# Five buffers instead of three for raw weights, and one place in SBUF for two sets of tiles, in a top-k attention kernel with two MLPs

## The chip, the cores and the metric

The kernel runs on one core of a Trainium2 chip. The metric is device time in microseconds (us), lower is better. The engines are TensorE (PE, with its weight loads as PEld), VectorE (DVE), ScalarE (ACT), GpSimd (POOL) and SyncE (SP); in this kernel SP issues all DMAs from one queue, in order, and each engine works through its own instructions in order.

## The reference, cut to what matters

Attention over 4 batches, 8 heads, 576 positions of 64 values, in which each row of scores keeps its 32 largest entries; then two MLPs (512 to 2048 to 512) on the 2304 rows that come out. All values are float32.

```python
scores = scale * np.matmul(q, k.transpose(0, 1, 3, 2))
kth = np.partition(scores, -32, axis=-1)[..., -32:-31]
scores = np.where(scores >= kth, scores, -1e9)
attn = softmax(scores)
x = np.matmul(attn, v)                      # laid out as 2304 rows of 512
h = x @ w_in;   x = (h - np.tanh(h)) @ w_out        # first MLP
h = x @ w_in2;  x = elu(h) @ w_out2                 # second MLP
```

## The kernel before, in words

The 2304 rows are cut into six chunks of 384. For each chunk the kernel computes eight groups of attention tiles (48 groups in all) and then the chunk's two MLPs in 32 steps (m is the MLP, ft one of 16 slices of 128 hidden columns). The attention of chunk c+1 runs beside the MLPs of chunk c. A group's scores are matmuls into PSUM (L332 to L335) that ACT copies out (L336); the top 32 of each row are found on DVE in four rounds of MAX8 (L357) and three of MATCH_REPLACE8 (L371), and one DVE instruction masks and sums (L378). PE transposes the result (L399), ACT copies it (L400), PE multiplies with v (L421). A step of an MLP is `first` (matmuls h, L528, then on ACT the tanh, L531, or the relu and exp, L533 and L534), `gate` (g on DVE, L542 or L547, then `split` into a high and a low part gh and gl, on ACT and POOL, L140 and L141) and `second` (matmuls acc, L564).

**Raw weights.** The weights arrive as 64-bit words that each hold two float32 values, and they are prepared once, on the way into chunk 0. `prepare` (L166) takes one half of one (m, ft): 128 x 512 raw words, 4 KB in each of 128 partitions, 512 KB in all. It loads them into a tile `raw` (L171 and L172, named wr in the trace; three buffers, RAW_BUFS); ACT scales and rounds the low words (L182), POOL multiplies (L184), ACT scales the high words (L186, or L181 into a PSUM bank while that is free, which holds for the first 22 of the 64 halves); DVE joins both into `w` (L187, named wf, two buffers), which is the last reader of `raw`; ACT and POOL split `w` into a weight tile (L191, named wp; 5 buffers for half 0, 6 for half 1), and the weight tile is stored to DRAM (L192). From chunk 1 on the prepared weights are loaded from there (L203). Eight (m, ft), 12 to 19, are prepared early, and chunk 0 loads them from DRAM as well (EARLY, PREP_AT, PREP_RATE); the other 24 are prepared in the order in which chunk 0 needs them, and their weight tiles go straight to PE.

**Parked groups.** While chunk 0's attention runs alone, the scores of groups 16 to 23 are computed as well and parked in DRAM (`park`, L307: tile `s`, named sp, two buffers; its q and k in qp and kp, one buffer each), to be loaded again when their turn comes. `park` is traced with a lowered priority (`later`).

**The order of the work.** The program is written in ticks, four to a group. `before`, `mid`, `late` and `ends` say in which tick the loads, the scores, the transposes and the rest of a group are written; chunk 0's MLPs begin in tick 36, and each step writes one `load_next`, which is either `prepare` or a load of prepared weights. That order gives priorities only: a planner (TileContext with a simulated timeline) takes the written instructions by priority, hands out the buffers of each tag, and lays down the fixed order of every engine's queue and the waits. An instruction can come long before its tick where its data and buffers are free by the planner's simulation, so preparation runs ahead as far as its buffers let it.

Tiles live in SBUF pools. Before the change all of them but two constants lie in one pool, `sb`, each tag with its own place for the whole program.

Of the kernel before, what the change touches and what calls it, by code (L numbers as in the profile page):

```python
# [19 lines left out]
P = 128  # L20
B, H, S, D = 4, 8, 576, 64
# [7 lines left out]
NF = DFF // P  # L29
# [14 lines left out]
NMAX = max(SIZES)  # L44
# [7 lines left out]
EARLY = range(12, 20)  # L52
PREP_AT = 8
PREP_RATE = 2.5
AHEAD = 6

PARTED = 2
# [11 lines left out]
PARK_BUFS = 2  # L69
# [2 lines left out]

WI_BUFS = 5
WO_BUFS = 6
RAW_BUFS = 3
G_BUFS = 3
T_BUFS = 3
QR_BUFS = 2
KR_BUFS = 2
# [8 lines left out]
G_BUFS = 3  # L88
T_BUFS = 3
# [9 lines left out]
NU = 384  # L99
# [8 lines left out]
def tile_topk_attention_two_mlps(  # L108
# [9 lines left out]
    nc = tc.nc  # L118

    def pool(name, bufs, space=None):  # L120
        kw = {} if space is None else {"space": space}
        return ctx.enter_context(tc.tile_pool(name=name, bufs=bufs, **kw))

    const = pool("const", 1)
    sb = pool("sb", 2)
    ps = pool("ps", 1, PSUM)
    dr = pool("dr", 1, DRAM)

# [20 lines left out]
    def bank(tag, name, bufs):  # L149
        return ps.tile([P, 512], F32, tag=tag, name=name, bufs=bufs)  # L150
# [8 lines left out]
    weights, loads = {}, [(ci, m, ft) for ci in range(len(SIZES)) for m in range(2) for ft in range(NF)]  # L159

    def weight_tile(half, name):
        return sb.tile([P, 2, 512], F32R, tag=f"w{half}", name=name, bufs=(WI_BUFS, WO_BUFS)[half])

    stage = {"at": 0, "wide": True}

    def prepare(m, ft, half):  # L166

        raw = sb.tile([P, 512], I64, tag="wr", name=f"wr{m}_{ft}_{half}", bufs=RAW_BUFS)  # L171
        nc.sync.dma_start(raw, (w1, w2)[m][ft][:, half * 512 : half * 512 + 512])  # L172
        words = raw.bitcast(F32).rearrange("p (n w) -> p n w", w=2)
        w = sb.tile([P, 512], F32, tag="wf", name=f"wf{m}_{ft}_{half}", bufs=2)
        low, scaled = words.bitcast(U32)[:, :, 0], words[:, :, 1]
        small = scaled
        if "wide" in stage:
            small = bank(f"acc{stage['at'] % 3}", f"sc{m}_{ft}_{half}", 1)
            stage["at"] += 1
        if small is not scaled:  # L180
            nc.scalar.activation(small, scaled, copy, scale=2.0**-112)  # L181
        nc.scalar.activation(low.bitcast(I32), low, copy, scale=2.0**-29 * (1 - 2.0**-20), bias=-0.5 + 7.5 * 2.0**-20)  # L182
        top = raw.bitcast(FP16).rearrange("p (n w) -> p n w", w=4)[:, :, 1]
        nc.gpsimd.tensor_mul(top, scaled, tiny)  # L184
        if small is scaled:
            nc.scalar.activation(scaled, scaled, copy, scale=2.0**-112)  # L186
        nc.vector.scalar_tensor_tensor(  # L187
            w.bitcast(U32), small.bitcast(U32), 3, low, op0=ALU.logical_shift_left, op1=ALU.bitwise_or
        )
        wt = weight_tile(half, f"wp{m}_{ft}_{half}")  # L190
        split(wt[:, 0], wt[:, 1], w)  # L191
        nc.sync.dma_start(f(scratch[m, ft, half]), f(wt))  # L192
        return wt

    def load_next():
        if loads:
            ci, m, ft = loads.pop(0)
            for half in range(2):
                if ci == 0 and m * NF + ft not in EARLY:
                    weights[ci, m, ft, half] = prepare(m, ft, half)  # L200
                    continue
                wt = weights[ci, m, ft, half] = weight_tile(half, f"wt{ci}_{m}_{ft}_{half}")
                newest["weights"] = nc.sync.dma_start(f(wt), f(scratch[m, ft, half]))  # L203
# [10 lines left out]
    for ci, size in enumerate(SIZES):  # L214
        for p in range(NPAIR):
            row = []
            c0 = 0
            for b, q0, n in CHUNKS[ci]:
                for heads in ([[0], [1]] if n >= 256 else [[0, 1]]):
                    u = Unit()  # L220
# [18 lines left out]
            for us in cuts:  # L239
                g = Group()  # L240
# [19 lines left out]
    def parked(u):  # L260

        return u.g.at in PARK

    def load_q(u):
        u.qraw = sb.tile([P, NU], F32, tag="qp" if parked(u) else "qraw", name=f"qraw{u.id}", bufs=1 if parked(u) else QR_BUFS)
        src = qT[u.b, 2 * u.p + u.heads[0] : 2 * u.p + u.heads[-1] + 1, :, u.q0 : u.q0 + u.n].rearrange("h d s -> d h s")
        nq = u.n * len(u.heads)
        for half in range(1 if u.whole or parked(u) else 2):
            nc.sync.dma_start(u.qraw[half * D : half * D + D, :nq].rearrange("d (h s) -> d h s", s=u.n), src)

    def load_k(u):
        u.kraw = {}
        for h in u.heads:
            u.kraw[h] = sb.tile([P, S], F32, tag="kp" if parked(u) else "kraw", name=f"kraw{u.id}_{h}", bufs=1 if parked(u) else KR_BUFS)
# [31 lines left out]

    def park(u, t):  # L307

        s = sb.tile([P, S], F32, tag="sp", name=f"sp{u.id}_{t}", bufs=PARK_BUFS)
        products(u, t, s, True)  # L310
        u.parked[t] = dr.tile([P, S], F32, tag=f"sd{u.id}_{t}", name=f"sd{u.id}_{t}")
        nc.sync.dma_start(u.parked[t], s)
# [204 lines left out]
    def first(ci, m, ft):  # L517
        n = SIZES[ci]
        xh, xl = x_tiles[ci] if m == 0 else z_tiles[ci]
        h = bank("h", f"h{ci}_{m}_{ft}", 2)[:, :n]  # L520
        wv = weights.pop((ci, m, ft, 0)).rearrange("p a (k c) -> p a k c", c=P)
        jobs = [(wi, xs, kt) for wi, xs in ((0, xh), (1, xh), (0, xl)) for kt in range(4)]
        if m == 0 and ft == 0:
            jobs.sort(key=lambda x: x[2])
        late = (n // P - 1) * P
        for cs in (slice(0, late), slice(late, n)) if m == 1 and ft < PARTED and late else (slice(0, n),):
            for a, (wi, xs, kt) in enumerate(jobs):
                nc.tensor.matmul(h[:, cs], wv[:, wi, kt], xs[:, kt, cs], start=(a == 0), stop=(a == len(jobs) - 1))  # L528
        t = sb.tile([P, NMAX], F32, tag="t", name=f"t{ci}_{m}_{ft}", bufs=T_BUFS)[:, :n]
        if m == 0:  # L530
            nc.scalar.activation(t, h, AF.Tanh)  # L531
        else:
            nc.scalar.activation(t, h, AF.Relu, scale=-1.0)  # L533
            nc.scalar.activation(t, t, AF.Exp, scale=-1.0)  # L534
        parts[ci, m, ft] = h, t

    def gate(ci, m, ft):
        n = SIZES[ci]
        h, t = parts[ci, m, ft]
        g = sb.tile([P, NMAX], F32, tag="g", name=f"g{ci}_{m}_{ft}", bufs=T_BUFS)[:, :n]  # L540
# [7 lines left out]
        gh = sb.tile([P, NMAX], F32R, tag="gh", name=f"gh{ci}_{m}_{ft}", bufs=G_BUFS)[:, :n]  # L548
        gl = sb.tile([P, NMAX], F32R, tag="gl", name=f"gl{ci}_{m}_{ft}", bufs=G_BUFS)[:, :n]
        newest["gates"] = split(gh, gl, g)  # L550
        parts[ci, m, ft] = gh, gl

# [49 lines left out]
    def step_parts(i):  # L602

        ci, m, ft = steps[i]
        nxt = steps[i + 1] if i + 1 < len(steps) else None
        turn = m == 0 and ft == NF - 1
        early = nxt is not None and not turn

        def a():
            if early:  # L610
                first(*nxt)

        def b():
# [12 lines left out]

        return a, b, c
# [53 lines left out]
    early = list(EARLY)  # L681
    for tick in range(FIRST_TICK, n_ticks):
        for do in before.get(tick, ()):
            do()
        while early and PREP_AT + PREP_RATE * (len(EARLY) - len(early)) <= tick:
            i = early.pop(0)
            for half in range(2):
                prepare(i // NF, i % NF, half)
        if starts[0] - AHEAD <= tick < starts[0]:
            load_next()  # L690
# [10 lines left out]
        at, r = divmod(tick, 4)  # L701
# [63 lines left out]
```

## Time and profile before

| what | value |
|---|---|
| median of 3 runs (lowest to highest) | 1243.47 us (1241.08 to 1243.83) |
| the profiled execution's own time | 1242.22 us |
| its span, first to last instruction | 1240.4 us |
| mean granted TensorE clock, share of full speed | 0.970 |
| PE busy | 1186.0 us (96%) |
| DVE busy | 974.2 us (79%) |
| ACT busy | 765.2 us (62%) |
| POOL busy | 585.7 us (47%) |
| DMA: moved, mean rate | 300.73 MB, 242 GB/s |
| loads of raw weights | 64 of 512 KB |

A busy share is the time in which the engine had an instruction running, over the span. PE's matmuls overlap and their ends are modelled, so that a PE shown as busy may still be slow. A releaser is the instruction or transfer whose end let a waiting engine go on. The DMA share is the mean busy share of the core's 16 DMA engines. The span is 1.8 us shorter than the execution's own time.

### The profile page before, as it was taken

The numbers are of one execution on the slowest core, as the hardware profiler recorded it, in microseconds if no ns is written. First come the engines' busy times: TensorE is split into PE (matmuls) and PEld (weight loads), VectorE is DVE, ScalarE is ACT, GpSimd is POOL, SyncE is SP. The second block draws the span as 40 slices with busy tenths as digits, with TensorE's granted clock in tenths as the row PEclk, the third lists the DMA queues.
The fourth block names the chain that finished last, engine by engine and source line by source line (L and its number), as shares of the span: only waits on it lengthen the run. The fifth ranks groups of instructions, "written<-read, shape, count | busy, mean of one in ns | idle before, by whom it ended". The sixth has DMA issues, their size and how long they took to land.

```text
span 1240.4 us, 19710 instructions
## 1 busy us (share of the span) xinstructions
PE 1186.0 (96%) x6349; PEld 993.3 (80%) x6349; DVE 974.2 (79%) x1951; ACT 765.2 (62%) x1670; POOL 585.7 (47%) x613
## 2 busy tenths in 40 slices
PE   6799989999998999999999999999999999999998
PEld 4455558888767887888988989989998988889887
DVE  7989999999999999978879679899789997100111
ACT  5999988788785434656556556566565564432333
POOL 4676549978984222244423345435344413333221
PEclk9995699998999999999999999999999999999999
DMA  8999627896979995778887778788778566687672
GB/s 261 330 332 308 229 81 255 295 347 210 312 266 347 328 274 144 238 212 280 206 199 236 240 219 261 218 265 223 239 241 247 197 169 196 204 283 251 218 255 78
DMA packets 114888, 300.73 MB, mean 242 GB/s; under 512 B 22496, under 2 KB 39776, under 8 KB 114784
## 3 DMA queue, kind: packets, MB, share of 16 engines
q1 hardware_dynamic: 114784, 299.46, 76.8%
q8 instruction: 51, 0.84, 0.3%
q14 instruction: 53, 0.43, 0.1%
HBM read 254.02 MB, written 45.39 MB: 241 GB/s over the span
## 4 chain that ended last, share of the span: by engine, by line
PE 71%; DVE 12%; ACT 6%; DMA 6%; issue 2%; POOL 1%; SPq 0%; ACTq 0%; DVEq 0%; POOLq 0%
PE h L528 27%; PE acc L564 27%; PE av L421 5%; PE pt L399 4%; DVE vm L357 4%; DMA wr<-in_w_dram 4%; DVE w L371 4%; PE ps L332 2%; PE pp L332 2%; PE ps L334 2%; PE ps L335 2%; DVE e L378 2%; DVE wf L187 1%; DMA kraw<-in_kT_dram 1%; DMA s<-sd 1%
## 5 line engine op out<-in xcount | busy, mean ns | idle before, releaser
L141 POOL TENSOR_TENSOR gl<-g,gh 128x384 fp32r<-128x384 f32 x192 | 207.7, 1083 | 376.2 <-ACT gh L140 355.0
L357 DVE MAX8 vm<-w 128x8 f32<-128x576 f32 x432 | 316.3, 749 | 3.2
L564 PE MATMUL acc<-wt,gh 128*128 128x512 f32 x1008 | 268.9, 398 | 0.3 <-ACT gh L140 0.3
L564 PEld LDWEIGHTS acc<-wt,gh 128*128 128x128 f32 x1008 | 185.6, 189 | 34.5 <-issue 2.7
L371 DVE MATCH_REPLACE8 w<-vm,w 128x576 f32<-128x576 f32 x288 | 212.9, 740 | 0.0
L140 ACT ACTIVATE gh<-g 128x384 fp32r<-128x384 f32 x192 | 100.6, 525 | 82.3 <-DVE g L542 43.3
L528 PE MATMUL h<-zh,wt 128*128 128x384 f32 (+2 forms) x768 | 146.8, 327 | 3.5 <-DVE g L542 2.4
L564 PE MATMUL acc<-wt,gl 128*128 128x512 f32 x504 | 147.9, 398 | 0.0
L542 DVE SCALAR_TENSOR_TENSOR g<-t,h 128x384 f32<-128x384 f32 x96 | 52.2, 544 | 117.9 <-ACT t L534 115.5
L357 DVE MAX8 vm<-s 128x8 f32<-128x576 f32 x144 | 107.4, 750 | 45.1 <-ACT s L336 42.5
L528 PE MATMUL h<-xh,wt 128*128 128x384 f32 x672 | 141.1, 339 | 0.1
L399 PE MATMUL pt<-ident,e 128*116 128x128 f32 (+1 forms) x720 | 118.5, 293 | 18.2 <-ACT s L336 6.4
L336 ACT ACTIVATE s<-ps 128x288 f32<-128x288 f32 (+1 forms) x272 | 106.5, 411 | 45.2 <-PE ps L335 36.5
L528 PEld LDWEIGHTS h<-zh,wt 128*128 128x128 f32 x768 | 125.7, 191 | 9.8 <-DVE g L542 2.7
L400 ACT ACTIVATE ph<-pt 116x384 f32<-116x384 f32 (+1 forms) x240 | 110.2, 496 | 32.7 <-PE pt L399 31.8
L399 PEld LDWEIGHTS pt<-ident,e 128*116 128x116 f32 (+1 forms) x720 | 89.7, 143 | 45.3 <-ACT s L336 9.6
L528 PEld LDWEIGHTS h<-xh,wt 128*128 128x128 f32 x672 | 117.3, 188 | 7.4 <-DVE w L371 1.2
L533 ACT ACTIVATE t<-h 128x384 f32<-128x384 f32 x96 | 46.7, 488 | 118.8 <-PE h L528 118.7
L184 POOL TENSOR_TENSOR wr<-wr,tiny 128x512 f16<-128x512 f32 x64 | 92.4, 1449 | 43.5 <-ACT wr L182 29.5
L378 DVE SCALAR_TENSOR_TENSOR e<-s,vm,e 128x576 f32<-128x576 f32 x115 | 109.3, 955 | 2.2 <-ACT e L361 1.5
L564 PEld LDWEIGHTS acc<-wt,gl 128*128 128x128 f32 x504 | 92.5, 188 | 18.2
L371 DVE MATCH_REPLACE8 w<-vm,s 128x576 f32<-128x576 f32 x144 | 106.7, 741 | 0.0
(83 smaller groups left out, 2002.2 us busy)
## 6 DMA issues: line engine op xcount, KB each, us to landing
wt<-w SPq DMA_DIRECT2D x336, 512.0 KB, 5.1
wr<-in_w_dram SPq DMA_DIRECT2D x64, 512.0 KB, 5.4
w<-wp SPq DMA_DIRECT2D x64, 512.0 KB, 5.5
kraw<-in_kT_dram SPq DMA_DIRECT2D x112, 144.0 KB, 4.9
vraw<-in_vL_dram SPq DMA_DIRECT2D x64, 160.0 KB, 3.4
qraw<-in_qT_dram SPq DMA_DIRECT2D x80, 96.0 KB, 4.8
sd<-sp SPq DMA_DIRECT2D x24, 288.0 KB, 5.3
s<-sd SPq DMA_DIRECT2D x24, 288.0 KB, 5.7
```

The lines of the kernel that those rows point to most:

```text
L140: nc.scalar.activation(hi, src, copy)
L141: return nc.gpsimd.tensor_sub(lo, src, f(hi))
L184: nc.gpsimd.tensor_mul(top, scaled, tiny)
L336: nc.scalar.activation(s[lo:hi, cs], pt[lo:hi, :HS], copy)
L357: nc.vector.max(g.vm[:, j, min(r, 1)], u.s[t] if r == 0 else g.w[j])
L371: nc.vector.match_replace(g.w[j], v, u.s[t] if r == 0 else g.w[j], FILL)
L378: nc.vector.scalar_tensor_tensor(u.e[t], u.s[t], v[:, 7:8], u.e[t], op0=ALU.is_ge, op1=ALU.mult, accum_out=g.sum[:, j : j + 1])
L399: nc.tensor.transpose(pt[:kn, j * P : j * P + P], v.e[t][:, k0 : k0 + kn], ident)
L400: nc.scalar.activation(g.ph[:kn, blk, :nq], pt[:kn, :nq], copy)
L421: nc.tensor.matmul(banks[c0][h * D : h * D + D, : v.n], v.vraw[h][:kn, blk], v.g.ph[:kn, blk, cs], start=(blk == order[0]), stop=(blk == o ...
L528: nc.tensor.matmul(h[:, cs], wv[:, wi, kt], xs[:, kt, cs], start=(a == 0), stop=(a == len(jobs) - 1))
L564: nc.tensor.matmul(acc[ci, m][t], gx[:, t * P : t * P + P], wt[:, wi], start=(ft == 0 and k == 0), stop=(ft == NF - 1 and k == 2),)
```

## The change

RAW_BUFS goes from 3 to 5, which takes 2 x 4 KB more in each partition. Room for it comes from tiles that are not alive at the same time: the tiles of the first stretch alone (qp, kp, sp: 8448 bytes per partition) move into a pool of their own, `op`, which is closed when the first tile of an MLP is asked for; the MLPs' tiles t, g, gh, gl (18432 bytes) move into a pool `mlp` that is opened then and takes over the same place. `prepare` is cut in three functions with the same instructions in the same order; the tile `w` is asked for later in it. OPEN_BUFS is 0, so that no raw tile ever lies in the pool `op`.

```diff
+OPEN_BUFS = 0
...
-RAW_BUFS = 3
+RAW_BUFS = 5
...
     sb = pool("sb", 2)
+    opening = ExitStack()
+    pools = {"open": opening.enter_context(tc.tile_pool(name="op", bufs=1))}
+
+    def mlp_tile(shape, dt, **kw):
+        if "open" in pools:
+            opening.close()
+            del pools["open"]
+            pools["mlp"] = pool("mlp", 1)
+        return pools["mlp"].tile(shape, dt, **kw)
...
+        early = "wide" in stage
+        at = stage["raw"] = stage["raw"] + 1
+        if early and at % (RAW_BUFS + OPEN_BUFS) >= RAW_BUFS:
+            raw = pools["open"].tile([P, 512], I64, tag="wo", name=f"wr{m}_{ft}_{half}", bufs=OPEN_BUFS)
+        else:
+            raw = sb.tile([P, 512], I64, tag="wr", name=f"wr{m}_{ft}_{half}", bufs=RAW_BUFS)
         nc.sync.dma_start(raw, (w1, w2)[m][ft][:, half * 512 : half * 512 + 512])
+        words_of(m, ft, half, raw)
+
+    def words_of(m, ft, half, raw):
+
         words = raw.bitcast(F32).rearrange("p (n w) -> p n w", w=2)
-        w = sb.tile([P, 512], F32, tag="wf", name=f"wf{m}_{ft}_{half}", bufs=2)
...
+        join(m, ft, half, small, low)
+
+    def join(m, ft, half, small, low):
+
+        w = sb.tile([P, 512], F32, tag="wf", name=f"wf{m}_{ft}_{half}", bufs=2)
...
         wt = weight_tile(half, f"wp{m}_{ft}_{half}")
+        if m * NF + ft not in EARLY:
+            weights[0, m, ft, half] = wt
         split(wt[:, 0], wt[:, 1], w)
         nc.sync.dma_start(f(scratch[m, ft, half]), f(wt))
-        return wt
...
-        u.qraw = sb.tile([P, NU], F32, tag="qp" if parked(u) else "qraw", ...
+        u.qraw = (pools["open"] if parked(u) else sb).tile([P, NU], F32, tag="qp" if parked(u) else "qraw", ...
...
-        s = sb.tile([P, S], F32, tag="sp", name=f"sp{u.id}_{t}", bufs=PARK_BUFS)
+        s = pools["open"].tile([P, S], F32, tag="sp", name=f"sp{u.id}_{t}", bufs=PARK_BUFS)
...
-        t = sb.tile([P, NMAX], F32, tag="t", name=f"t{ci}_{m}_{ft}", bufs=T_BUFS)[:, :n]
+        t = mlp_tile([P, NMAX], F32, tag="t", name=f"t{ci}_{m}_{ft}", bufs=T_BUFS)[:, :n]
...
```

The tiles kp, g, gh and gl are changed in the same way as qp and t.

## Rows read from the trace of the kernel before

**Rows 1.** Windows: stretch, busy us (instructions) of PE, PEld, DVE, ACT, POOL; PEclk, DMA share, GB/s.

```profile
0.00:30.00 30.00, 20.56 (x41) 13.21 (x42) 21.76 (x43) 17.01 (x38) 12.74 (x17) 1.00 0.80 261
30.00:100.00 70.00, 59.72 (x154) 34.33 (x153) 60.37 (x117) 62.75 (x140) 47.37 (x53) 0.91 0.94 323
100.00:160.00 60.00, 56.12 (x179) 31.76 (x179) 58.42 (x115) 55.48 (x131) 36.42 (x43) 0.62 0.77 259
160.00:280.00 120.00, 111.87 (x674) 96.14 (x673) 120.00 (x236) 99.74 (x217) 94.96 (x97) 0.97 0.73 250
280.00:400.00 120.00, 108.06 (x627) 90.79 (x626) 119.35 (x227) 92.62 (x194) 94.83 (x87) 0.97 0.81 280
400.00:500.00 100.00, 96.94 (x537) 80.85 (x536) 97.70 (x209) 43.72 (x89) 24.62 (x31) 0.98 0.87 254
500.00:1100.00 600.00, 598.09 (x3458) 526.00 (x3457) 481.33 (x982) 346.66 (x771) 235.12 (x250) 1.00 0.77 226
```

**Rows 2.** The tile wr: engine, operation, count, min/median/max ns, first to last start (us).

```profile
L172 SPq DMA_DIRECT2D wr<-in_w_dram x64: 327/338/1274, 5.6 to 369.5; - x64
L182 ACT ACTIVATE wr<-wr x64: 645/676/733, 12.0 to 375.7; 128x512 int32<-128x512 uint32 x64
L184 POOL TENSOR_TENSOR wr<-wr,tiny x64: 1337/1370/1955, 12.8 to 376.5; 128x512 f16<-128x512 f32 x64
...
L187 DVE SCALAR_TENSOR_TENSOR wf<-wr x42: 666/976/1759, 107.4 to 381.1; 128x512 uint32<-128x512 uint32 x42
...
DMA to landing us min/median/max: 3.6/5.4/11.1
```

**Rows 3.** Timeline of DVE, 296 to 345 us (start, us, instruction): one join.

```profile
303.34 0.67 DVE L187 SCALAR_TENSOR_TENSOR wf<-wr 128x512 uint32<-128x512 uint32 x1
```

**Rows 4.** Timeline of SP's queue, 300 to 345 us: the raw load behind that join.

```profile
304.04 0.33 SPq L172 DMA_DIRECT2D wr<-in_w_dram  x1
```

**Rows 5.** Timeline of SP's queue, 130 to 200 us: raw loads and the last parked store.

```profile
137.41 0.53 SPq L172 DMA_DIRECT2D wr<-in_w_dram  x1
...
148.55 0.54 SPq L312 DMA_DIRECT2D sd<-sp  x1
189.50 1.26 SPq L172 DMA_DIRECT2D wr<-in_w_dram  x2
```

**Rows 6.** Timeline of ACT, 170 to 192 us: the first tanh.

```profile
182.43 0.88 ACT L531 ACTIVATE t<-h 128x384 f32<-128x384 f32 x2
```

**Rows 7.** Waits of ACT, 160 to 400 us: total us, times, longest us.

```profile
ACT wr L182 <- DMA wr<-in_w_dram: 13.4, 13, 1.9
```

**Rows 8.** Waits of PE, 160 to 400 us: the two longest groups.

```profile
PE pt L399 <- ACT ph L400: 3.5, 3, 1.7
PE ps L334 <- ACT s L336: 3.1, 5, 1.5
```

**Rows 9.** The chain that ended last, 300 to 350 us (start, us, what): raw loads in it.

```profile
310.42 5.01 DMA wr<-in_w_dram
...
323.68 6.20 DMA wr<-in_w_dram
...
335.14 6.39 DMA wr<-in_w_dram
```

**Rows 10.** Waits of ACT, 0 to 160 us.

```profile
ACT sc L181 <- DMA wr<-in_w_dram: 10.0, 7, 2.5
...
ACT wr L182 <- DMA wr<-in_w_dram: 2.1, 2, 1.9
```

**Rows 11.** Waits of DVE, 0 to 160 us.

```profile
DVE vm L357 <- ACT s L336: 11.5, 7, 5.7
DVE wf L187 <- POOL wr L184: 5.3, 4, 2.1
```

**Rows 12.** Windows of 20 us with the most bytes moved (columns as in the first group).

```profile
20.00:40.00 20.00, 10.76 (x21) 5.45 (x19) 18.52 (x38) 13.11 (x29) 12.47 (x14) 1.00 0.99 343
...
240.00:260.00 20.00, 20.00 (x112) 18.23 (x112) 20.00 (x43) 15.33 (x34) 13.88 (x17) 0.98 1.02 376
```

More of the change, by code (lines that the diff above doesn't have):

```diff
@@ L162, in weight_tile @@
         return sb.tile([P, 2, 512], F32R, tag=f"w{half}", name=name, bufs=(WI_BUFS, WO_BUFS)[half])
-    stage = {"at": 0, "wide": True}
+    stage = {"at": 0, "wide": True, "raw": -1}
     def prepare(m, ft, half):
-        raw = sb.tile([P, 512], I64, tag="wr", name=f"wr{m}_{ft}_{half}", bufs=RAW_BUFS)
+        early = "wide" in stage
[4 more added lines that the diff above has]
+            raw = sb.tile([P, 512], I64, tag="wr", name=f"wr{m}_{ft}_{half}", bufs=RAW_BUFS)
         nc.sync.dma_start(raw, (w1, w2)[m][ft][:, half * 512 : half * 512 + 512])
+        words_of(m, ft, half, raw)
+    def words_of(m, ft, half, raw):
         words = raw.bitcast(F32).rearrange("p (n w) -> p n w", w=2)
-        w = sb.tile([P, 512], F32, tag="wf", name=f"wf{m}_{ft}_{half}", bufs=2)
         low, scaled = words.bitcast(U32)[:, :, 0], words[:, :, 1]
         small = scaled
-        if "wide" in stage:
+        early = "wide" in stage
+        if early:
             small = bank(f"acc{stage['at'] % 3}", f"sc{m}_{ft}_{half}", 1)
             stage["at"] += 1
-        if small is not scaled:
-            nc.scalar.activation(small, scaled, copy, scale=2.0**-112)
-        nc.scalar.activation(low.bitcast(I32), low, copy, scale=2.0**-29 * (1 - 2.0**-20), bias=-0.5 + 7.5 * 2.0**-20)
+        if True:
+            if small is not scaled:
+                nc.scalar.activation(small, scaled, copy, scale=2.0**-112)
+            nc.scalar.activation(low.bitcast(I32), low, copy, scale=2.0**-29 * (1 - 2.0**-20), bias=-0.5 + 7.5 * 2.0**-20)
         top = raw.bitcast(FP16).rearrange("p (n w) -> p n w", w=4)[:, :, 1]
@@ L186, in prepare @@
             nc.scalar.activation(scaled, scaled, copy, scale=2.0**-112)
-        nc.vector.scalar_tensor_tensor(
-            w.bitcast(U32), small.bitcast(U32), 3, low, op0=ALU.logical_shift_left, op1=ALU.bitwise_or
-        )
+        join(m, ft, half, small, low)
+    def join(m, ft, half, small, low):
+        w = sb.tile([P, 512], F32, tag="wf", name=f"wf{m}_{ft}_{half}", bufs=2)
+        if True:
+            nc.vector.scalar_tensor_tensor(
+                w.bitcast(U32), small.bitcast(U32), 3, low, op0=ALU.logical_shift_left, op1=ALU.bitwise_or
+            )
         wt = weight_tile(half, f"wp{m}_{ft}_{half}")
+        if m * NF + ft not in EARLY:
+            weights[0, m, ft, half] = wt
         split(wt[:, 0], wt[:, 1], w)
         nc.sync.dma_start(f(scratch[m, ft, half]), f(wt))
-        return wt
     def load_next():
@@ L199, in load_next @@
                 if ci == 0 and m * NF + ft not in EARLY:
-                    weights[ci, m, ft, half] = prepare(m, ft, half)
+                    prepare(m, ft, half)
                     continue
@@ L264, in load_q @@
     def load_q(u):
-        u.qraw = sb.tile([P, NU], F32, tag="qp" if parked(u) else "qraw", name=f"qraw{u.id}", bufs=1 if parked(u) else QR_BUFS)
+        u.qraw = (pools["open"] if parked(u) else sb).tile([P, NU], F32, tag="qp" if parked(u) else "qraw", name=f"qraw{u.id}", bufs=1 if parked(u) else QR_BUFS)
         src = qT[u.b, 2 * u.p + u.heads[0] : 2 * u.p + u.heads[-1] + 1, :, u.q0 : u.q0 + u.n].rearrange("h d s -> d h s")
@@ L273, in load_k @@
         for h in u.heads:
-            u.kraw[h] = sb.tile([P, S], F32, tag="kp" if parked(u) else "kraw", name=f"kraw{u.id}_{h}", bufs=1 if parked(u) else KR_BUFS)
+            u.kraw[h] = (pools["open"] if parked(u) else sb).tile([P, S], F32, tag="kp" if parked(u) else "kraw", name=f"kraw{u.id}_{h}", bufs=1 if parked(u) else KR_BUFS)
             for half in range(1 if u.whole or parked(u) else 2):
@@ L539, in gate @@
         h, t = parts[ci, m, ft]
-        g = sb.tile([P, NMAX], F32, tag="g", name=f"g{ci}_{m}_{ft}", bufs=T_BUFS)[:, :n]
+        g = mlp_tile([P, NMAX], F32, tag="g", name=f"g{ci}_{m}_{ft}", bufs=T_BUFS)[:, :n]
         if m == 1:
@@ L547, in gate @@
             nc.vector.tensor_sub(g, h, t)
-        gh = sb.tile([P, NMAX], F32R, tag="gh", name=f"gh{ci}_{m}_{ft}", bufs=G_BUFS)[:, :n]
-        gl = sb.tile([P, NMAX], F32R, tag="gl", name=f"gl{ci}_{m}_{ft}", bufs=G_BUFS)[:, :n]
+        gh = mlp_tile([P, NMAX], F32R, tag="gh", name=f"gh{ci}_{m}_{ft}", bufs=G_BUFS)[:, :n]
+        gl = mlp_tile([P, NMAX], F32R, tag="gl", name=f"gl{ci}_{m}_{ft}", bufs=G_BUFS)[:, :n]
         newest["gates"] = split(gh, gl, g)
```

## The prediction

> **What bounds the kernel now.** I read the busy times in windows first, because the whole-span shares hide that three stages have different limits [rows 1]. From 500 us on PE is busy 598 of 600 us at full clock and DVE only 481: PE is the bound, and nothing about raw weights lies there. What the change can give must therefore come from before 500 us, and it comes through to the end if PE reaches its full stretch earlier. From 160 to 400 us, when chunk 0's MLPs run beside chunk 1's attention and the last 35 halves are joined, PE is idle for 8.1 + 11.9 = 20.1 us, and its clock stands at 0.97; DVE is busy for 239.35 of 240 us. From 30 to 160 us, attention alone with preparation beside it, everything is nearly full: ACT 62.75 of 70 us, DVE 58.42 of 60, the DMA engines 94% and then 77%, and PE spends the second part at a clock of 0.62.
>
> A full DVE from 160 to 400 us looks like a proof that DVE is the bound there. It is not quite one: after 500 us DVE needs only 481 of 600 us, so top-k work that it does early is work it need not do later. What counts is PE's loss.
>
> Next I read the raw tile [rows 2] and the timelines. A half is held from its load to its join: 5.4 us to land, 0.68 on ACT, 1.37 on POOL, another ACT pass of the same size as L182, 0.98 for the join, 9.1 us without any queueing. A join ends at 303.34 + 0.67 = 304.01 us [rows 3] and a raw load is issued at 304.04 [rows 4]: the load waited for a buffer and for nothing else. With three buffers the loads go out at (137.4 - 5.6) / 31 = 4.3 us apiece up to 137 us and (369.5 - 189.5) / 31 = 5.8 us apiece afterwards [rows 2, 5]; between 137.41 and 189.50 us none goes out at all, since the weight tiles are full until the MLPs begin and the raw buffers with them [rows 5].
>
> Last I read who pays. ACT works in order, and with only three buffers its pass L182 is often at the head of its queue before its data is there: it stands still for a raw load 13 times between 160 and 400 us, 13.4 us together [rows 7]. Behind it are queued the copies of the transposes and of the scores, and the two longest groups of PE's waits in that stretch are for just these (3.5 and 3.1 us) [rows 8]. The chain that ended last runs through three raw loads in a row there, 5.01 + 6.20 + 6.39 = 17.6 us [rows 9]. In the first 160 us ACT stands 10.0 + 2.1 us for raw loads [rows 10] and DVE 5.3 us for POOL's pass on raw words [rows 11].
>
> **The change part by part.** No instruction is added or taken away; the number of bytes moved stays. The cut of `prepare` into three functions and the later request for `w` cost nothing: the same operations go to the same engines.
>
> Step a, the stretch from 160 to 400 us. With five buffers a load can be issued two joins earlier, about 2 x 5.8 = 11.6 us. A wait of at most 1.9 us is covered by that, so I expect nearly all of ACT's 13.4 us to go. What of it reaches PE? Between nothing (DVE's order holds everything) and 13.4 us (of the 20.1 us that PE idles). PE's longest waits are on ACT, but DVE's full queue shares in them, so I take half: 6.5 us. What is late next is POOL, 190 of 240 us busy, and DVE.
>
> Step b, the pause from 137 to 189 us. Two more halves can be loaded and worked on in place. That takes 2 x 1.37 us of POOL's work and about 2.7 us of ACT's out of the busy stretch after 180 us and puts them into a pause. Between 0 and 2.7 us; POOL is only 79% busy afterwards, so I take 1.
>
> Step c, the opening. DVE's 5.3 us for POOL's pass: 1.2 us or so belong to the very first half, which no buffer helps; of the remaining 4.1 I take half, 2 us, since the DMA engines are 94% busy from 30 to 100 us and a load that is issued earlier can't land much earlier. Bounds: 4.1 us gained, and on the other side the loss that the second rival prices.
>
> For step c the trace shows 343 GB/s at a busy share of 0.99 from 20 to 40 us, but 376 GB/s from 240 to 260 us [rows 12]. The Trainium skill (DMA: Bandwidth & Descriptors, Specifications) gives an HBM limit of about 358 GB/s per core; by that rule the opening is at its ceiling, step c gives nothing, and the sum would be 2 us smaller. The window at 376 GB/s is above that limit, and the trace decides: not a hard ceiling here.
>
> Step d, the queues that the loads are moved past. SP's queue is in order: a raw load at its head, waiting for a buffer, holds back the stores and the loads of q and k behind it, so fewer of those waits is a small plus; each load still costs 0.34 us to issue. I count 0.
>
> Step e, the shared place. This adds a wait: the first tile t of the MLPs, written by the first tanh on ACT, now needs qp, kp and sp to be given back. The last parked store is issued at 148.55 us [rows 5]; with a landing as slow as the slowest raw load, 11.1 us [rows 2], it is done by 160 us, and the tanh runs at 182.43 [rows 6]. 22 us of cover: cost 0. If the cover were gone, ACT would stand at that tanh with the copies of scores behind it, and each us would be lost one for one.
>
> The planner lays all queues down anew, so the order of unrelated instructions moves as well. The trace can't show that; I bound it by 3 us either way, about a sixth of PE's idle time from 160 to 400 us, and take 0.
>
> **The sum**: 6.5 + 1 + 2 = 9.5 us, from the profiled execution's 1242.2 us: 1232.7. The median of the runs is 1.25 us above that execution, so the forecast for the median is 1234.0 us. From 500 us on nothing gives this back as long as DVE has slack, and it has 119 us of it between 500 and 1100 us. A difference of 0.2%, 2.5 us, is about what a measurement of this kernel can tell from none.
>
> **The rivals.** First, **no difference**: the queue of DVE sets the pace from 160 to 400 us, ACT's waits for raw loads were time that ACT had to spare (it is 80% busy there), and PE's idle time stays and only changes its releaser. For it: DVE's 239.35 of 240 us. Against it: the three loads in the chain. Left are steps b and c at about half: 1242 us.
>
> Second, **slower**: in the opening two more loads of 512 KB are in flight ahead of each load of q and k on the same queue. At 323 GB/s [rows 1] each takes 524 KB / 323 GB/s = 1.6 us, so that k lands up to 3.2 us later. Six of chunk 0's eight groups have their loads in that traffic: 19 us at the most; if two or three of them are caught, 6.5 to 10 us, less 3 for what step a still gives, which is about 1249 us. It decides from the point where DVE's wait for scores, 11.5 us now [rows 11], grows by more than the steps give, that is to above 20 us. Against it: 5.7 of the 11.5 us is the start, and k is asked for several ticks ahead.
>
> Third, **more**: ACT's waits pass to PE in full, and PE, busier, loses less of its clock. 13.4 + 2.7 + 4.1 = 20.2 us; PE's clock of 0.97 over 240 us is worth 0.03 x 240 = 7.2 us on top at the most. About 1220 us, with 1216 as the end.
>
> Fourth, **the shared place does not come free in time**: the planner, with other work ready earlier, pushes the parked groups (lowered priority) past the first tanh. They need to slip by over 22 us. If they slip by 30, the loss is about 8 us and most of the gain is left: near 1242. Little speaks for it.
>
> **How the numbers follow.** The forecast, 1228 to 1240 us: 0.56. More, below 1228: 0.18. No difference, 1241 to 1246: 0.13, the fourth rival in it. Slower, above 1246: 0.13. So faster by over 0.2%: 0.74, within 0.2%: 0.13, slower: 0.13. The range of 8 in 10 reaches from 1222 (a third of the third rival's chance lies lower) to 1247, leaving out about 0.06 below and 0.12 above.
>
> **What would show each step right or wrong.** Step a: ACT's waits for raw loads from 160 to 400 us fall from 13.4 us to under 4, raw loads vanish from the chain there, PE's idle time falls from 20 us to about 13, and chunk 0's second MLP ends earlier. If ACT's waits go and PE's idle time stays, the first rival is right. Step b: after about 140 us five raw halves instead of three stand loaded. Step c: DVE's 5.3 us shrink, and its wait for scores stays near 11.5. Step e: the first tanh starts right behind its matmuls. The forecast is wrong if PE's busy share from 500 us on drops, which would mean that the gain was handed back there.

## The result, and the profile after

The change takes the median from 1241.36 us (1239.92 to 1243.83, 6 runs) to 1232.06 us (1229.88 to 1232.36, 6 runs): a ratio of 0.9917 (of the means of the runs, 1231.46 to 1241.73 us), 95% interval 0.9903 to 0.9931, or 9.3 us less by the medians. The forecast was 9.5 us less. The profiled execution took 1232.15 us, close to the median, with a span of 1230.4 us; the lines of the changed kernel below are from it. The experiments ran on several chips, so each one's ratio is against runs of the kernel before on the same chip; stretches of profiled executions are also laid side by side across chips, and there small differences are not read.

The windows of the changed kernel (stretch, busy us and instructions of PE, PEld, DVE, ACT, POOL, then PEclk, DMA share, GB/s), to be laid beside [rows 1]:

```profile
0.00:30.00 30.00, 23.46 (x46) 14.48 (x47) 22.50 (x45) 20.49 (x45) 17.08 (x20) 1.00 0.89 292
30.00:100.00 70.00, 58.15 (x154) 32.09 (x154) 68.36 (x138) 67.58 (x154) 54.01 (x61) 0.85 1.00 368
100.00:160.00 60.00, 56.94 (x190) 31.98 (x188) 56.52 (x109) 52.06 (x125) 29.09 (x36) 0.66 0.60 204
160.00:280.00 120.00, 114.34 (x684) 97.42 (x682) 118.11 (x229) 98.69 (x214) 97.50 (x98) 0.97 0.78 266
280.00:400.00 120.00, 113.82 (x658) 97.88 (x658) 119.23 (x225) 90.20 (x191) 93.50 (x85) 0.97 0.85 295
400.00:500.00 100.00, 96.61 (x537) 79.68 (x534) 97.14 (x210) 45.78 (x97) 24.34 (x30) 0.98 0.75 233
500.00:1100.00 600.00, 598.08 (x3452) 525.85 (x3451) 476.75 (x975) 345.05 (x765) 233.80 (x252) 1.00 0.77 228
```

Three things are to be seen. From 30 to 100 us DVE is busy 8.0 us longer than before and POOL 6.6 us longer: preparation has moved forward, out of the 60 us that follow, where POOL falls by 7.3. From 160 to 400 us PE is idle 5.7 + 6.2 = 11.8 us, where it was 20.1. From 500 us on PE's busy time is the same to a hundredth.

The waits of ACT and of PE from 160 to 400 us in the changed kernel (total us, times, longest us), which answer to [rows 7] and [rows 8]:

```profile
ACT wr L206 <- POOL wr L204: 10.5, 14, 2.0
ACT t L558 <- PE h L555: 7.6, 5, 3.1
...
ACT wr L202 <- DMA wr<-in_w_dram: 5.0, 5, 1.8
```

```profile
PE pt L426 <- ACT s L363: 2.8, 3, 1.7
PE ps L361 <- ACT s L363: 2.5, 3, 1.6
PE acc L591 <- POOL gl L151: 2.2, 4, 1.0
```

ACT's wait for raw loads has gone from 13.4 to 5.0 us. A wait for POOL's pass on the same half has taken its place at the head of ACT's list. In the chain that ended last, two raw loads are left between 160 and 400 us:

```profile
241.43 12.81 DMA wr<-in_w_dram
...
346.08 4.19 DMA wr<-in_w_dram
```

They make 12.81 + 4.19 = 17.0 us. In the kernel before it is the three loads of [rows 9] and one more in the same 240 us, 21.4 us in all:

```profile
216.05 3.84 DMA wr<-in_w_dram
```

**Where the time came from.** Three events cut the program into stretches in either kernel: the end of chunk 0's attention (the last part of x, xl on DVE), the end of its first MLP (y on ACT) and the end of its second MLP (o on ACT). Their rows in the kernel before, then in the changed one (engine, operation, count, min/median/max ns, first to last start in us):

```profile
L507 DVE TENSOR_TENSOR xl<-xun,xh x1: 553/553/553, 178.7 to 178.7; 128x384 fp32r<-128x384 f32 x1
...
L578 ACT ACTIVATE y<-acc x3: 592/600/604, 271.5 to 272.5; 128x512 f32<-128x512 f32 x3
...
L597 ACT ACTIVATE o<-acc x3: 592/601/602, 394.4 to 395.8; 128x512 f32<-128x512 f32 x3
```

```profile
L534 DVE TENSOR_TENSOR xl<-xun,xh x1: 548/548/548, 172.3 to 172.3; 128x384 fp32r<-128x384 f32 x1
...
L605 ACT ACTIVATE y<-acc x3: 592/598/603, 268.5 to 269.5; 128x512 f32<-128x512 f32 x3
...
L624 ACT ACTIVATE o<-acc x3: 596/600/607, 381.2 to 382.1; 128x512 f32<-128x512 f32 x3
```

| stretch | before, us | after, us | difference |
|---|---|---|---|
| to the end of the attention | 178.7 | 172.3 | -6.4 |
| first MLP | 92.8 | 96.2 | +3.4 |
| second MLP | 122.9 | 112.7 | -10.2 |
| from there to the end of the span | 846.0 | 849.2 | +3.2 |
| sum: the span | 1240.4 | 1230.4 | -10.0 |

Two stretches win 16.6 us and two give 6.6 of it back. In the second MLP's stretch DVE is nearly full in both kernels. Its windows there, with MAX8 alone behind each (one top-k round of one tile each), before and after:

```profile
271.50:394.40 122.90, 110.96 (x674) 93.11 (x674) 122.25 (x229) 96.01 (x201) 99.67 (x93) 0.97 0.82 279
...
271.50:394.40 122.90, 44.97 (x63) 0.97 0.82 279
```

```profile
268.50:381.20 112.70, 106.52 (x658) 91.39 (x658) 111.41 (x206) 93.12 (x197) 95.05 (x89) 0.97 0.82 284
...
268.50:381.20 112.70, 40.83 (x58) 0.97 0.82 284
```

DVE has not become faster there: 206 instructions in 112.7 us are the same pace as 229 in 122.9. The count inside a shorter stretch is smaller in any case, so it proves nothing by itself. What tells is all that DVE does from the start of the program to the end of the second MLP, before and after:

```profile
0.00:394.40 394.40, 350.72 (x1638) 261.24 (x1639) 374.31 (x721) 323.18 (x707) 285.21 (x292) 0.91 0.80 272
```

```profile
0.00:381.20 381.20, 347.91 (x1624) 257.31 (x1625) 365.92 (x702) 321.48 (x707) 285.68 (x291) 0.90 0.81 282
```

The MLP ends 13.2 us earlier. 8.4 us of that is work that DVE has not yet done (702 instructions instead of 721), and 4.8 us is time in which DVE stood idle before (20.1 us) and does not now (15.3). What it leaves out it does later, where [rows 1] and the last windows above show that it has slack. That is another order of work, and the experiments were made to tell it from fewer waits.

### The profile page after: what moved, and what is told of

Its sections match the earlier page's. It is cut to its first block, busy times and chain, and to the rows that moved or that the text cites. A ratio compares the mean times of both kernels' runs of the same rounds, so it can differ in the third digit from the quotient of the medians.

```text
span 1230.4 us, 19712 instructions
## 1 busy us (share of the span) xinstructions
PE 1186.0 (96%) x6349; PEld 990.3 (80%) x6349; DVE 972.7 (79%) x1951; ACT 763.2 (62%) x1670; POOL 584.3 (47%) x613
## 4 chain that ended last, share of the span: by engine, by line
PE 74%; DMA 7%; ACT 6%; DVE 6%; POOL 3%; issue 3%; SPq 0%; ACTq 0%; POOLq 0%; DVEq 0%
PE h L555 28%; PE acc L591 28%; PE av L448 5%; PE pt L426 5%; DMA wr<-in_w_dram 3%; DVE w L398 2%; DVE vm L384 2%; PE ps L361 2%; PE ps L362 2%; PE pp L359 1%; DMA kraw<-in_kT_dram 1%; PE ps L359 1%; POOL wr L204 1%; DVE wf L213 1%; DMA s<-sd 1%
## 5 line engine op out<-in xcount | busy, mean ns | idle before, releaser
L405 DVE SCALAR_TENSOR_TENSOR e<-s,vm,e 128x576 f32<-128x576 f32 x115 | 106.8, 932 | 1.7 <-ACT e L388 1.2
```

The costliest lines, as they stand in the source:

```text
L405: nc.vector.scalar_tensor_tensor(u.e[t], u.s[t], v[:, 7:8], u.e[t], op0=ALU.is_ge, op1=ALU.mult, accum_out=g.sum[:, j : j + 1])
```

## The experiments

Two theories stood at first. **Waits**: with five buffers a load can be issued two joins earlier, ACT stands less and PE stands less (step a of the prediction). **Rival**: the time comes from the opening, or from the shared place, or from nothing but a new order in the queues. Diffs are against the changed kernel.

### The shared place alone

```diff
-RAW_BUFS = 5
+RAW_BUFS = 3
```

> The change with three raw buffers: only the shared place is left of it. Prediction's theory (step e costs nothing, all of the gain comes from the buffers): within 2.5 us of the kernel before, about 1241. Rival (the place, or the new way in which tiles wait for it, moves the time): more than 3 us away on either side, and the first tanh late behind the last parked store.

Measured: 1.0009 (0.9992 to 1.0026), 1241.43 us against 1240.8. Every queue has the order of the kernel before here, so that the run times the shared place and nothing else. Within its interval it costs nothing, and it brings nothing by itself. Its profiled execution is also a yardstick. With the same order as before, the attention ends at 180.8 us (178.7 before) and the second MLP at 397.6 (394.4), while each of the stretches behind the attention differs by 0.6 us at most. Differences of that size between two profiled executions show nothing.

### Five buffers in one part of the preparation

Five for the first 22 halves, three from there on:

```diff
-OPEN_BUFS = 0
+OPEN_BUFS = 2
...
-RAW_BUFS = 5
+RAW_BUFS = 3
```

> Five raw buffers for the first 22 halves alone (two of them in the opening's pool), three for the other 42. Prediction's theory: this is step c alone, 2 us of gain, about 1239. Rival A (the opening is where the gain is born, since chunk 0's MLPs began 6.8 us earlier in the changed kernel): about 1235, 6 to 7 us. Rival B (an earlier start is given back, since chunk 0's second MLP began only 2.3 us earlier): 0 to 3 us.

Measured: 0.9985 (0.9971 to 1.0000), 1239.5 us against 1240.8. The attention ends at 172.4 us, as early as in the changed kernel, but the second MLP ends at 392.7 us. The opening's gain is lost again in the stretch that has three buffers.

Three for the first 32 halves, five from there on:

```diff
-RAW_BUFS = 5
+RAW_BUFS = 3
+LATE_BUFS = 2
...
-        if early and at % (RAW_BUFS + OPEN_BUFS) >= RAW_BUFS:
-            raw = pools["open"].tile([P, 512], I64, tag="wo", name=f"wr{m}_{ft}_{half}", bufs=OPEN_BUFS)
+        if at >= 32 and at % (RAW_BUFS + LATE_BUFS) >= RAW_BUFS:
+            raw = mlp_tile([P, 512], I64, tag="wl", name=f"wr{m}_{ft}_{half}", bufs=LATE_BUFS)
```

> Three raw buffers for the first 32 halves, five from there (two of them in the MLPs' pool). Prediction's theory: steps a and b without c, 7.5 us of gain, about 1234, with ACT's waits for raw loads from 160 to 400 us under 6 us and PE's idle time near 12. Rival A (the gain is born in the opening): no more than 3 us of gain, about 1238 or above.

Measured: 1.0050 (1.0033 to 1.0068), 1247.58 us against 1240.8: slower, which neither theory expected. Two more buffers in just the stretch in which ACT stood for loads went with a slower kernel. The attention ends at 180.9 us here, no later than with the shared place alone (180.8). The edit does more than add buffers: they lie in the pool `mlp`, so that `op` is closed when the first of them is asked for and not at the first tanh. Two raw loads go out at 150.2 and 150.5 us, just behind the last parked store, in a pause in which the kernel before has none. The run does not show what later buffers alone are worth.

Three for the first 40, five for the last 24, with the raw loads kept in the order in which they are written:

```diff
-RAW_BUFS = 5
+RAW_BUFS = 3
+LATE_BUFS = 2
...
+        if at >= 40 and at % (RAW_BUFS + LATE_BUFS) >= RAW_BUFS:
+            raw = sb.tile([P, 512], I64, tag="wl", name=f"wr{m}_{ft}_{half}", bufs=LATE_BUFS)
...
-        nc.sync.dma_start(raw, (w1, w2)[m][ft][:, half * 512 : half * 512 + 512])
+        with behind("raw"):
+            newest["raw"] = nc.sync.dma_start(raw, (w1, w2)[m][ft][:, half * 512 : half * 512 + 512])
```

> Three raw buffers for the first 40 halves (all of the early ones and of the first MLP), five for the last 24, all loads kept in their order. Theory now (the second half of chunk 0's MLPs is limited by the pace of the raw loads, whatever happens before): the stretch from the middle of chunk 0's MLPs to chunk 1's first tanh shrinks from 104 to about 95 us and the time falls by 5 to 8 us, 1233 to 1236. Rival A (late buffers are worth nothing without the faster opening): 1239 to 1242. Rival B (a mixed supply makes the planner lay the queues worse, as with five from the 32nd half): 1244 or above.

Measured: 0.9989 (0.9974 to 1.0004), 1242.28 us against 1243.1. The second MLP takes 117.6 us instead of 122.9, yet the whole is no shorter. Five buffers in one part of the preparation keep the gain in none of the three runs, each of which also has its queues laid anew.

### Four buffers

```diff
-RAW_BUFS = 5
+RAW_BUFS = 4
```

> Four raw buffers. If the gain is latency that is covered bit by bit: about half of the 9.3 us, 1236 to 1238. If the first buffer more covers most of it (ACT's waits for a load are 1.9 us at the longest, and a load goes out one join, about 5.8 us, earlier): 7 to 9 us, 1232 to 1234. If the planner's new order of the queues is what pays, and the buffers only let it: anywhere between 1230 and 1243, not between the two kernels.

Measured: 0.9935 (0.9914 to 0.9955), 1232.41 us against 1240.8, most of the gain. Its waits of ACT from 160 to 400 us:

```profile
ACT wr L202 <- DMA wr<-in_w_dram: 18.0, 12, 4.0
```

ACT stands 18.0 us for raw loads, longer than before the change, and the kernel is still about 8 us faster. This is the run that step a does not survive: the length of that wait is not what the loads cost.

### No extra halves in the pause

The loads from the 33rd half on are queued behind the store of the first half of m = 0, ft = 5, so that the pause of step b holds no more halves than it did:

```diff
-        nc.sync.dma_start(raw, (w1, w2)[m][ft][:, half * 512 : half * 512 + 512])
+        with behind("stored") if at >= 32 else nullcontext():
+            nc.sync.dma_start(raw, (w1, w2)[m][ft][:, half * 512 : half * 512 + 512])
...
-        nc.sync.dma_start(f(scratch[m, ft, half]), f(wt))
+        stored = nc.sync.dma_start(f(scratch[m, ft, half]), f(wt))
+        if m == 0 and ft == 5 and half == 0:
+            newest["stored"] = stored
```

> Five raw buffers, but the loads from the 33rd half on are queued behind the store of the first weight tile that had to wait for the MLPs, so that none of them goes out in the pause. Prediction's theory (step b is worth 1 us): 1233. Rival (the two halves loaded in the pause are what carries the gain of the opening through the first MLP, since five buffers in the opening alone lost it there): 1236 to 1240.

Measured: 0.9925 (0.9906 to 0.9944), 1234.1 us against 1243.1. The interval overlaps that of the changed kernel, so that step b is small; the planner lays the queues differently for this edit too, and the two intervals can't tell 1 us from none or from 3. ACT's wait for raw loads is 15.8 us here, longer than before the change, and nearly the whole gain is there.

### Another order at the same buffers

PARK_LOW is how far the priority of the parked groups is lowered. Another value lays the queues anew and adds no instruction. With three buffers:

```diff
-PARK_LOW = 300
+PARK_LOW = 500
...
-RAW_BUFS = 5
+RAW_BUFS = 3
```

> Three raw buffers, and the parked groups' priority lowered by 500 instead of 300, which makes the planner lay several hundred instructions of each queue in another order; no work, no buffer differs. If a new order alone is worth 5 us or more either way, this lies below 1237 or above 1246, and the comparison of single kernels proves little. If buffers decide: 1239 to 1244.

Measured: 1.0054 (1.0037 to 1.0070), 1250.78 us against 1243.1. With five:

```diff
-PARK_LOW = 300
+PARK_LOW = 200
```

> Five raw buffers, and the parked groups' priority lowered by 200 instead of 300: another order of the queues with the same buffers. If buffers decide: 1230 to 1235. If a new order alone is worth 5 us or more: below 1228 or above 1236.

Measured: 1.0061 (1.0043 to 1.0079), 1251.65 us against 1243.1. Five buffers in another order are slower than three in the old one, and by the two ratios about 1.4% behind the same five in the changed kernel's order. Its windows from 100 to 160 us and from 400 to 500 us:

```profile
100.00:160.00 60.00, 54.63 (x155) 29.87 (x154) 52.86 (x99) 46.33 (x108) 25.39 (x33) 0.57 0.61 191
...
400.00:500.00 100.00, 93.72 (x502) 77.35 (x501) 93.40 (x201) 41.22 (x85) 22.70 (x30) 0.95 0.81 219
```

DVE stands still for 7.1 of 60 us in the first, and PE's granted clock averages 0.57 there, near its lower level (1.2 GHz), against 0.66 in the changed kernel; its attention ends at 178.2 us, and the rest of the program after the second MLP takes 855.1 us where the changed kernel takes 849.2. Against the kernel before the loss lies behind the second MLP: that ends at 394.6 us (394.4 before), and the rest is 9.1 us longer. Its preparation runs as early as the changed kernel's in the opening, with the 22nd half's pass on ACT at 79.7 us, and its last raw load goes out at 356.8 us, also earlier than before; so early preparation does not make a kernel faster by itself.

### The order held fixed

Five buffers, and every queue (SP's too) held in the order of the kernel before, by ordering edges between neighbours that add no wait:

```diff
+def keep_order(tc):
...
+        for a, b in zip(names, names[1:]):
+            tc.add_manual_dep(traced[b], a, edge, reason="order")
...
         tile_topk_attention_two_mlps(tc, *args)
+        keep_order(tc)
```

> Five raw buffers, and every engine's queue and SP's held in exactly the order of the kernel before, by ordering edges between neighbours that add no wait; only the raw loads no longer wait for the join three halves back. Prediction's step a (ACT's standing for raw loads is the price, and buffers alone take it away): ACT's waits for raw loads from 160 to 400 us well under 13.4 us and the time at 1233 to 1237. Rival (the gain is the new order that the planner lays when it has the buffers): 1239 to 1243, even if ACT's waits shrink.

Measured: 0.9987 (0.9971 to 1.0002), 1240.73 us against 1242.73. The waits move the way that the prediction said, but not as far. SP, which waited 27.0 us for joins in the kernel before (first fence, 0 to 400 us), waits 5.5 us for them (second fence, first line). ACT's wait from 160 to 400 us falls from 13.4 to 9.8 us (second fence, second line). The held queue of SP still issues each load behind the same transfers, and the last one goes out at 366.1 us instead of 369.5.

```profile
SPq L172 <- DVE wf L187: 27.0, 24, 3.3
```

```profile
SPq L327 <- DVE wf L353: 5.5, 7, 2.1
...
ACT wr L342 <- DMA wr<-in_w_dram: 9.8, 12, 1.7
```

Its windows from 160 to 400 us:

```profile
160.00:280.00 120.00, 110.15 (x667) 94.03 (x667) 120.00 (x231) 97.22 (x212) 96.01 (x98) 0.99 0.77 257
280.00:400.00 120.00, 106.58 (x616) 90.00 (x615) 120.00 (x227) 92.19 (x192) 93.80 (x85) 0.97 0.81 282
```

None of it brings time that could be told from none: DVE is busy in all of the 240 us, and PE no more than before. The run shows that the buffers without a new order do not carry the gain. It does not show that ACT's waits cost nothing: 3.6 us of them went, at the prediction's price of a half that is 1.8 us, and the ratio says 1.6 us, with an interval from none to 3.6.

The same five buffers, the changed kernel's order up to 175 us and the order of the kernel before from there on (the same edges, another list):

```diff
+ORDER = (
...
         tile_topk_attention_two_mlps(tc, *args)
+        keep_order(tc)
```

> Five raw buffers; up to the start of chunk 0's MLPs (175 us of the changed kernel's trace) every queue is held in the changed kernel's order, and what is left after that in the order of the kernel before. If the order of the opening is the gain (old order throughout gave 0.9987, new order throughout 0.9917): 0.990 to 0.994, 1230 to 1235. If the new order after the MLPs' start is needed to keep it: 0.996 to 0.999, 1237 to 1241, with the opening's gain at the end of chunk 0's top-k and lost by the end of chunk 0's MLPs.

Measured: 0.9949 (0.9930 to 0.9968), 1237.66 us against 1244.04. The attention ends at 173.2 us, the second MLP at 389.6. ACT's wait for raw loads and the windows, both from 160 to 400 us, in that kernel:

```profile
ACT wr L342 <- DMA wr<-in_w_dram: 11.5, 12, 2.0
```

```profile
160.00:280.00 120.00, 114.26 (x707) 98.61 (x705) 117.89 (x231) 97.98 (x215) 95.77 (x96) 0.99 0.77 251
280.00:400.00 120.00, 106.67 (x607) 89.38 (x608) 118.99 (x225) 91.00 (x190) 92.85 (x85) 0.97 0.83 291
```

The three kernels with five buffers thus split the gain: 0.13% for buffers without a new order (the interval takes in none), 0.38% for the new order up to 175 us, 0.32% for the new order after it. The split is for parts added in this sequence: the new order was always run with its buffers. The intervals of the first two kernels just miss each other and those of the last two touch, so that each share is known to about 0.2% either way. In the windows the last part is plain: from 280 to 400 us PE is busy 106.67 us here, 113.82 in the changed kernel. So it is in DVE's work up to the second MLP's end:

```profile
0.00:389.60 389.60, 348.46 (x1638) 256.55 (x1639) 374.15 (x721) 320.55 (x706) 285.56 (x292) 0.91 0.81 276
```

With the new order up to 175 us DVE does the same 721 instructions ahead of that end as in the kernel before, and the 4.8 us by which that end comes earlier are almost all idle time of DVE (15.4 us instead of 20.1). The new order behind it then takes 19 instructions, 8.2 us of work, out of the way (365.92 us in the changed kernel).

### More of the same

A third buffer for the joined words, to let joins run further ahead:

```diff
-        w = sb.tile([P, 512], F32, tag="wf", name=f"wf{m}_{ft}_{half}", bufs=2)
+        w = sb.tile([P, 512], F32, tag="wf", name=f"wf{m}_{ft}_{half}", bufs=3)
```

> The changed kernel with three buffers instead of two for the joined words wf. If what is late next is the join waiting for POOL to free wf (0.5 to 2 us of DVE's waits): within 2 us of the changed kernel, 1230 to 1234. If the order laid with it matters more than the buffer: anything from 1225 to 1250.

Measured: 0.9947 (0.9929 to 0.9966), 1235.45 us against 1242.73: no better than the changed kernel. Its queues are laid anew as well, so that the run puts no price on the join's wait. Seven raw buffers in the first 22 halves:

```diff
-OPEN_BUFS = 0
+OPEN_BUFS = 2
```

> The changed kernel with two raw buffers more for the first 22 halves, in the opening's pool (seven then, five later). DVE's idle time up to the end of chunk 0's top-k fell from 19.4 to about 11.6 us with four and with five buffers. If that is the floor (5.8 us of it is the start): the same time as with five, 1230 to 1234. If raw loads still limit the opening: 2 to 5 us less. Rival from the prediction (more loads ahead of those of q and k delay the scores): 1236 or above, with DVE waiting longer for the copies of the scores.

Measured: 1.0012 (0.9993 to 1.0030), 1244.37 us against 1242.73. The whole gain is gone. DVE's wait for scores is 8.3 us there:

```profile
DVE vm L384 <- ACT s L363: 8.3, 4, 5.8
```

That is less than the 11.5 us of [rows 11], so that the prediction's second rival (loads of q and k held up) is not what happens; the attention ends at 179.1 us, and why was not settled.

### All kernels side by side

From the rows of xl, y and o, the windows from 0 us to the second MLP's end and ACT's waits from 160 to 400 us, each in one profiled execution. Three of these lie well off their kernel's median: five buffers in the old order 4 us above it, the shared place alone 4 us above, three in another order 6 us below.

| kernel | ratio | attention ends | second MLP, us | it ends | DVE busy until then | rest of the span | ACT's wait for raw loads |
|---|---|---|---|---|---|---|---|
| before | 1 | 178.7 | 122.9 | 394.4 | 374.3 | 846.0 | 13.4 |
| shared place alone | 1.0009 | 180.8 | 123.4 | 397.6 | 374.1 | 846.3 | 14.2 |
| changed | 0.9917 | 172.3 | 112.7 | 381.2 | 365.9 | 849.2 | 5.0 |
| five, none more in the pause | 0.9925 | 170.5 | 119.7 | 388.5 | 372.3 | 843.7 | 15.8 |
| four buffers | 0.9935 | 169.6 | 117.3 | 383.8 | 371.1 | 846.8 | 18.0 |
| five, three for wf | 0.9947 | 175.0 | 119.7 | 387.4 | 374.4 | 845.6 | 10.4 |
| five, new then old order | 0.9949 | 173.2 | 123.7 | 389.6 | 374.2 | 846.3 | 11.5 |
| five for 22 halves, then three | 0.9985 | 172.4 | 124.1 | 392.7 | 370.7 | 844.8 | 23.8 |
| five, old order | 0.9987 | 175.5 | 124.4 | 394.3 | 377.5 | 848.8 | 9.8 |
| three for 40 halves, then five | 0.9989 | 177.8 | 117.6 | 391.7 | 372.8 | 846.7 | 11.8 |
| seven for 22 halves, then five | 1.0012 | 179.1 | 118.6 | 391.1 | 376.1 | 851.3 | 7.8 |
| three for 32 halves, then five | 1.0050 | 180.9 | 121.0 | 399.0 | 375.9 | 847.3 | 12.7 |
| three, other order (PARK_LOW) | 1.0054 | 176.8 | 124.8 | 397.7 | 374.4 | 845.8 | 19.3 |
| five, other order (PARK_LOW) | 1.0061 | 178.2 | 118.6 | 394.6 | 374.8 | 855.1 | 14.5 |

ACT's wait goes with nothing in this table: the two shortest are in the fastest kernel (5.0) and in one that is no faster than before (7.8), and with 15.8 and 18.0 us most of the gain is there. An earlier end of the second MLP comes from DVE standing idle less, from less of its work ahead of that end, or from both, and some kernels give it back in the rest of the span. The changed and the new-then-old kernel, with the same buffers, differ in the second MLP by 11.0 us and only in the order.

## Why the prediction was right or wrong

**Direction and size were right, the reason for the largest term was not.** 9.5 us were forecast and 9.3 measured. That the two agree is luck and no proof of the sum: the largest term is not what the gain is made of, a smaller one was too small, and a term set at 0 carries most of it.

**Step a** ("ACT's standing passes half to PE", 6.5 us). Most signs that were named came: ACT's wait 13.4 to 5.0 us (under 4 was forecast), PE's idle time 20.1 to 11.8 us (about 13 was forecast), an earlier end of the second MLP. One did not: the raw loads did not vanish from the chain, 17.0 of 21.4 us are left. And the mechanism falls. With four buffers ACT waits 18.0 us, without the extra halves in the pause 15.8, and nearly the whole gain is there; with seven in the opening it waits 7.8 us and there is none. The signs were those of an earlier preparation as such, and did not tell fewer waits from another order. Whether the first rival is right in the old order, so that DVE's full queue sets the pace and ACT's waits cost nothing, is not shown, since most of these waits stayed there.

**The step that failed** is the one about the planner: "I bound it by 3 us either way ... and take 0". At the same number of buffers a new order alone moved the time by 0.54% (about 7 us, three buffers, PARK_LOW) and by about 1.4% (about 18 us, five buffers); and in the change itself the order, once the buffers are there, carries 0.70% of the 0.83%, about 8 of the 9 us. Buffers were costed as shorter waits in a fixed order. What they do here is let the planner place loads, passes and joins earlier in all queues, as the rows of the raw tile show against [rows 2] and against the first 22 halves on ACT in the kernel before (first line):

```profile
L181 ACT ACTIVATE sc<-wr x22: 609/633/674, 11.5 to 97.4; 128x512 f32<-128x512 f32 x22
```

```profile
L187 SPq DMA_DIRECT2D wr<-in_w_dram x64: 328/338/1313, 5.6 to 346.1; - x64
...
L201 ACT ACTIVATE sc<-wr x22: 614/646/715, 11.1 to 78.4; 128x512 f32<-128x512 f32 x22
```

The last load goes out at 346.1 us instead of 369.5, and the 22nd half's pass on ACT starts at 78.4 us instead of 97.4. That is what the buffers allow; the slower kernel with five buffers in another order has it too (356.8 and 79.7 us), so that it is not enough for the gain.

**Step b** (1 us) is in bounds. In the pause five halves stand loaded instead of three (34 loads are out and 29 joins done, where it was 32 and 29), and no raw load goes out from 116.48 to 183.28 us (SP's queue, changed kernel):

```profile
112.07 0.34 SPq L187 DMA_DIRECT2D wr<-in_w_dram  x1
...
116.48 0.38 SPq L187 DMA_DIRECT2D wr<-in_w_dram  x1
...
153.82 7.20 SPq L339 DMA_DIRECT2D sd<-sp  x3
183.28 2.10 SPq L187 DMA_DIRECT2D wr<-in_w_dram  x2
```

**Step c** (2 us) was too small. The opening loads go out every (116.5 - 5.6) / 33 = 3.4 us instead of 4.3, and the attention ends 6.4 us earlier. By the difference of the runs with the old order and with the new one up to 175 us, about 4.7 us (0.38%) of that reach the end of the program. With five buffers in the opening alone it is 0.15%, about the 2 us of the step, but there the opening had won as much and the later stretch lost it. DVE's wait for POOL's pass did shrink, from 5.3 us in [rows 11] to 0.8, and its wait for scores did not grow:

```profile
DVE vm L384 <- ACT s L363: 8.1, 4, 5.8
...
DVE wf L213 <- POOL wr L204: 0.8, 1, 0.8
```

So the second rival's mechanism is not there. From 30 to 100 us the DMA engines moved 368 GB/s, where they had moved 323. The Trainium skill (DMA: Bandwidth & Descriptors, Specifications) states about 358 GB/s of HBM bandwidth per core; read as a ceiling, it would have left step c nothing. The window lies above that figure, and the measurement decides.

**Step d** (0) stands as far as it was tried: SP's waits for joins fell from 27.0 to 5.5 us in the old order, and the time did not move by more than its interval. In the changed kernel they are even longer than before (0 to 400 us), against the step's "fewer of those waits", in a kernel that is faster all the same:

```profile
SPq L187 <- DVE wf L213: 34.4, 28, 3.0
```

**Step e** (0) stands: 1.0009 (0.9992 to 1.0026) for the shared place alone. The cover shrank all the same. The last parked store now goes out at 153.82 + 7.20 = 161.0 us at the latest, and the first tanh runs at 175.59 us:

```profile
175.59 0.88 ACT L558 ACTIVATE t<-h 128x384 f32<-128x384 f32 x2
```

**"From 500 us on nothing gives this back"** holds as far as its sign goes: PE is busy 598.08 of 600 us there, 598.09 before. But 3.2 us are handed back after the second MLP and 3.4 in the first, which the prediction had nowhere. The third rival's gain by TensorE's clock did not come: the granted clock averages 0.97 from 160 to 400 us in both kernels.

**What stays open**: why one order is good and another bad. The runs show that the order carries the gain and in which stretches, not a rule by which it could have been foretold. What DVE has ahead of the second MLP's end explains the changed kernel against the new-then-old one, but not every pair of the table. The losses with three buffers and then five, and with seven in the opening, are unexplained. The changed order with three buffers was not tried, so what that order is worth without the buffers is open.

## What to carry to other kernels

Where a planner lays the queues, a buffer count is a change of the whole order: ask what can be placed earlier and which full engine then has less ahead of the critical step, and give the re-laying a bound from runs at other settings (0.5 to 1.4% here) before any wait is added up. The length of a wait on an engine with time to spare is no price. To tell waits from order, run the new resource with the old order held, and look there whether the waits really went: an order that was laid for the old resource keeps part of them. Signs in the profile that both causes share prove neither.

## What the runs showed that was not expected

DMA moved 368 GB/s for 70 us on end in the changed kernel at a DMA share of 1.00, 14% more than before in the same stretch at 0.94; a rate near the 376 GB/s that [rows 12] had shown for 20 us was held here for 70. And ACT standing 18.0 us for raw loads, 4.6 us more than before, went with a kernel that is 0.65% faster (0.45 to 0.86%).
